# A Fourier and MLP kernel in fp32: casts of one chunk's z in later slots, accumulator copies ahead of a cast, and one block of stores split off per step

## The chip, the core and the metric

The kernel runs on one core of one Trainium2 chip. The core's engines are named here as the profile names them: PE multiplies matrices (PEld loads its stationary operand), DVE and ACT work on tiles element by element, POOL does a few small operations, and SP issues the transfers (DMAs). Each engine takes its instructions in the order in which they were written down, and waits at the head of its own queue for whatever that instruction still lacks. The metric is the device time of one execution in microseconds (us). Before the change it is 1434.35 us, the median of three runs (1433.13 to 1434.81).

## The reference

Two layer pairs, run twice, on x of 2048 rows by 512 columns. `A` mixes by Fourier matrices, `B` is a token shift with a two-layer MLP.

```python
def _A_ref(x, dft_seq_re, dft_seq_im, dft_hid_re, dft_hid_im):
    a = jnp.einsum("bsd,ed->bse", x, dft_hid_re)
    b = jnp.einsum("bsd,ed->bse", x, dft_hid_im)
    return jnp.einsum("ts,bse->bte", dft_seq_re, a) - jnp.einsum("ts,bse->bte", dft_seq_im, b)

def _B_ref(x, w1, w2, w3, w4):
    h = _gelu(_layernorm(x, axis=-1) @ w1)
    # four groups of 128 columns, shifted by +1, -1, +2, -2 rows -> hs
    x1 = x + hs @ w2
    h2 = _gelu(_layernorm(x1, axis=-1) @ w3) @ w4
    return x1 + h2

x = x + _A_ref(_layernorm(x), ...)   # layer 0
x = x + _B_ref(_layernorm(x), ...)
x = x + _A_ref(_layernorm(x), ...)   # layer 1
x = x + _B_ref(_layernorm(x), ...)
```

## The kernel before

**Precision.** Every product of two fp32 matrices is made of three matmuls: each operand is split into a high part (`hi`, a copy in the type fp32r) and a low part (`lo`, the value less its high part). `mm3` issues hi·hi, hi·lo and lo·hi into one accumulator. So each operand tile costs ACT one cast (the high part; `high`, L426, or L228, L231 and L235 for streamed weights) and DVE one subtraction (the low part; `low`, L429, or L245), and a product can start with its high parts but needs a low part at its second matmul.

**The Fourier half of a layer** works on four chunks `c` of 512 output rows. For each, `x_phase` and then `y_phase` stream pieces of the sequence matrix (`ws`, 512 KB each, tiles `raw`, four buffers) through a ring of four split tiles (`ring`, ring0f to ring3f their unsplit sums). In `y_phase` there are eight steps k, each with two items, `by1` (into accumulators PC and PD) and `by0` (into PB and PA). One step consumes one pair of pieces, and both items need both pieces (L234, a subtraction on DVE). The items run in the order k = 0 to 5, then 6 by1, 7 by1, 6 by0, 7 by0. A pair's two buffers come free when DVE has made the second item's sum, and only then may SP issue the pair after next. At the last `by1` the kernel makes im0 from PC (L517), adds to im1 (L468), casts im0 (`high(im0)`, L426) and copies PD into X1, which is part of the tile `tmp` (L523). After the loop ACT copies PB and PA into `tmp` or, in chunk 3, `beside` (L531, L533). A short hidden-dimension phase (`hid`, matmuls that read `rr`) follows chunk 3 directly.

**turned0.** In chunk 3's `y_phase` four normalised tiles of chunk 0 are transposed in blocks of 32 by DVE into `turned0` (at k = 0), stored by SP to the DRAM tile `zd` (`turn_out`: four DMAs of 256 KB, one for each block b), and loaded back as `zt0f` at k = 7 (`turn_in`, L609). The transposition is finished by the two trips together. Chunks 1, 2 and 3 get their z in the same manner later.

**by_pairs: the slots.** The first half of the MLP is 32 slots of twelve matmuls each, written out by hand. A slot is either `shifted` (z times w1, gelu on ACT at L655, cast of the gelu to `rg` at L658, its low part on DVE at L659) or `mixed` (`rg` times w2, drained by DVE at L677). A `mixed` slot takes the four `rg` of its chunk in the order 1, 3, 0, 2, so its last three matmul groups may need the `rg` made just ahead of it. Chunk 2's last `shifted` is slot 19, its first `mixed` slot 20; chunk 3's z (`zt1f`, split into `zt`) is first read in slot 23. What else runs beside a slot stands in two lists: `D(slot, ...)` is written ahead of the slot's own DVE or ACT work, `A(slot, ...)` behind it. In these lists are the casts of z (`z_highs`, `z_half`), norms (`norm3`, `ln1_of`, all L330), transposes (`turn3`, L594), stores of turned tiles (`turn_out`) and loads back (`bring`, L697; `b12`, `b22` for chunk 1). The lists alone set the order; no planner moves anything.

After the slots the MLP's second half runs over pairs of chunks, then the layer ends.

Of the kernel before, what the change touches and what calls it, by code (L numbers as in the profile page):

```python
# [14 lines left out]
S, D, F = 2048, 512, 1376  # L15
# [5 lines left out]
NC = S // CH  # L21
# [5 lines left out]
NB = P // B  # L27
# [16 lines left out]
def spectral_mlp_kernel(ctx: ExitStack, tc: tile.TileContext, x, ws, hs, w1, w2, w34, out):  # L44
# [15 lines left out]
    z3d = [dram.tile([D, CH], F32, name=f"z3d{i}") for i in range(NC)]  # L60
# [24 lines left out]
    def at(name, word, *shape, dtype=F32R):  # L85
        return nc.alloc_sbuf_tensor_at(name, [P, *shape], dtype, offset=base + 4 * word).ap()
# [11 lines left out]
    turned0 = at("turned0", 5 * AY, KD, CH, dtype=F32)  # L98
# [25 lines left out]
    def xt(j):  # L124
        return xs[j // 2][:, j % 2]
# [4 lines left out]
    count = {"mm": 0, "tmp": 0, "turn": 0}  # L130
# [24 lines left out]
    def y_order():  # L155
        order = [(k, kind) for k in range(NP) for kind in ("by1", "by0")]
        order[-3], order[-2] = order[-2], order[-3]
        return order
# [111 lines left out]
    def stream():  # L270
        i = state["use"]
        if i and items[i - 1][3] is None:
            state["done"] += 1
        state["use"] += 1
        prefetch()
        while state["two"] <= i:
            stage_two()
        return slots.pop(i)
# [137 lines left out]
    def mm_half(ps, a, slot, first, last):  # L416
        for i in range(2):
            w = slice(i * P, (i + 1) * P)
            mm3(ps[i], a[:, 0, w], a[:, 1, w], slot[:, 0], slot[:, 1], first, last)
# [5 lines left out]
    def high(tf):  # L425
        nc.scalar.copy(tf[0][:, :, 0], tf[1][:, :, 1])  # L426

    def low(tf):
        nc.vector.tensor_tensor(tf[0][:, :, 1], tf[1][:, :, 1], tf[0][:, :, 0].bitcast(F32), op=ALU.subtract)  # L429
# [37 lines left out]
    def add(o, a, b, op=ALU.add):  # L467
        nc.vector.tensor_tensor(o, a, b, op=op)  # L468

    def run_late(*names):  # L470
        for i in names:
            for f in late.pop(i, ()):
                f()
# [29 lines left out]
    def y_phase(c, hook):  # L503
        for k, kind in y_order():
            first, last = k == 0, k == NP - 1
            s = stream()
            if kind == "by1":
                hook(k)
                if k == 2:
                    run_late("y")  # L510
                if k == 4:
                    add(re0s, re0s, im1s)
                mm_half(PC, ay[k][:, 2], s[:, 0], first, last)
                mm_half(PD, ay[k][:, 0], s[:, 1], first, last)
                if last:
                    for i in range(2):
                        nc.vector.scalar_tensor_tensor(  # L517
                            im0s[:, i], PC[i], -1.0, im1s[:, i], op0=ALU.mult, op1=ALU.subtract
                        )
                    add(im1s, re0s, im0s)  # L520
                    high(im0)
                    for i in range(2):
                        nc.scalar.copy(X1[:, i], PD[i])  # L523
            else:
                if k == NP - 2:
                    low(im0)
                mm_half(PB, ay[k][:, 3], s[:, 1], first, last)
                mm_half(PA, ay[k][:, 1], s[:, 0], first, last)
        t = tmp if c < NC - 1 else beside
        for i in range(2):  # L530
            nc.scalar.copy(t[:, i], PB[i])  # L531
        for i in range(2):
            nc.scalar.copy(t[:, 2 + i], PA[i])  # L533
        late.update(
            {
                "im1-": [lambda: add(im1s, im1s, re1s, ALU.subtract)],
                "re1+": [lambda: add(re1s, re1s, t[:, 0:2]), lambda: high(re1)],
                "im1+": [lambda: add(im1s, im1s, X1), lambda: high(im1)],
                "re1": [lambda: low(re1)],
                "re0+": [lambda: add(re0s, re0s, t[:, 0:2])],  # L540
                "im1": [lambda: low(im1)],
                "re0++": [lambda: add(re0s, re0s, t[:, 2:4]), lambda: high(re0)],
                "re0": [lambda: low(re0)],
            }
        )
        if c < NC - 1:
            for i, names in enumerate((["im1-"], ["re1+"], ["im1+", "re1"], ["re0+", "im1"], ["re0++"], ["re0"])):
                late[i + 1] = [f for n in names for f in late.pop(n)]
# [43 lines left out]
    def turn_one(t, q, u):  # L592
        v = t.rearrange("p d (a q j) -> p d a q j", a=NB, q=TC)[:, :, :, q]
        nc.vector.transpose(v, blocks_of(u))  # L594

    def turn_out(t, to=None):

        if to is None:
            count["turn"] += 1
            to = zd[count["turn"] % 2]  # L600
        z = to.rearrange("(e i) t -> i e t", i=B)
        for b in range(NB):
            v = t[b * B : (b + 1) * B].rearrange("i d (a t) -> i (d a) t", a=NB)
            nc.sync.dma_start(z[:, :, b * P : (b + 1) * P], v)

# [90 lines left out]
    def b_in(c, half, to):  # L696
        nc.sync.dma_start(blkf[to][:, :, 1], z3d[c].rearrange("(h d p) t -> h p d t", h=2, p=P)[half])  # L697
# [13 lines left out]
    def z_half(c, i):  # L711
        return [t[c % 2][:, 2 * i : 2 * i + 2] for t in (zt, ztf)]

    def by_pairs(layer, zs, xin, dst):
# [14 lines left out]
        def D(slot, *fs):  # L729
            todo.setdefault((slot, 0), []).extend(fs)  # L730

        def A(slot, *fs):
            todo.setdefault((slot, 1), []).extend(fs)
# [5 lines left out]
        def u_stats(c, i, n=2):  # L739
            return lambda: mrs[c].extend(stats(x1s[c][i : i + n]))  # L740

        def add_u(c, *qs):
            return lambda: [add(xt(c * TC + q), xt(c * TC + q), x1s[c][q]) for q in qs]
# [13 lines left out]
        def turn3(t, c, *qs):  # L757
            return lambda: [turn_one(t, q, x1s[c][q]) for q in qs]
# [4 lines left out]
        def bring(c, half, to):  # L763
            return lambda: b_in(c, half, to)
# [13 lines left out]
        def z_highs(c):  # L778
            return lambda: [high(z_half(c, i)) for i in range(2)]
# [63 lines left out]
        sc0, sc1, sc2 = scratch  # L843
# [27 lines left out]
        D(14, turn(sc1, 3, 2, 3))  # L871
        A(14, lambda: turn_out(sc1))
        A(16, lambda: turn_in(ztf[1]))
        A(18, z_highs(3))
        D(21, lambda: low(z_half(3, 0)))
        D(22, lambda: low(z_half(3, 1)))

        D(6, u_stats(0, 0))
# [15 lines left out]
        D(18, add_u(1, 0, 1, 2))  # L894
        A(19, norm3(1, 0, 1, 2))
        D(19, u_stats(1, 3, 1))
        D(20, add_u(1, 3))
        D(20, turn3(sc2, 1, 0, 1, 2))
        A(20, norm3(1, 3))
        D(21, turn3(sc2, 1, 3))  # L900
        A(21, lambda: turn_out(sc2, z3d[1]))
        A(23, bring(1, 0, "12"), bring(1, 1, "22"))
        A(26, bring(0, 1, "t4"))
        D(26, sum_of("t1", "12", "t1"))
        A(27, highs("12", "22"))
# [107 lines left out]
        for pair in range(n_pairs):  # L1013
# [14 lines left out]
            if pair == 0:  # L1028
                t = tmp[:, 0:4]
# [16 lines left out]
            for i, names in enumerate((("11", "21"), ("12", "22"))):  # L1046
                for d in range(KD):
                    b = blk[names[d // 2]]
# [395 lines left out]
    for layer in range(LAYERS):  # L1444
# [4 lines left out]
        for c in range(NC):  # L1449
            if layer == 0 and c == 0:  # L1450
# [57 lines left out]
                def hook(i):  # L1508
                    k, odd = divmod(i, 2)
                    if not i:  # L1510
                        second_low(1)
                        xp_stats(1)
                        second_low(0)
                        state["two"] += 1
                        issue_dma()
                        state["limit"] = 4
                        prefetch()
                    state["limit"] = w_items[layer]
                    if not odd:
                        if k + 1 < NP:  # L1520
                            xp_norm(k + 1, 3)
                            xp_main(k + 1)
                        if not k:
                            xp_main_lows(1)
                    else:
                        if 0 < k < NP - 1:
                            xp_main_lows(k + 1)
                        if k + 2 < NP:
                            xp_stats(k + 2)
                        if k:  # L1530
                            xp_sums(k - 1)
                            xp_highs(k - 1, False)
                            xp_lows(k - 1, False)
                    w4_split(i)
# [46 lines left out]
            def hook(k):  # L1581
                if layer and c == 0:
                    for step, f in zip((1, 1, 2), (ay_sums, ay_highs, ay_lows)):
                        if k == step:
                            f(7)
                if k == 1 and c:
                    rows(X1, x1d, (c - 1) * TC + 2, 2, False)
                if c == NC - 1 and k == 0:
                    for q in range(TC):
                        turn_one(turned0, q, tmp[:, q])  # L1590
                if c == NC - 1 and k == 2:
                    turn_out(turned0)
                if c == NC - 1 and k == NP - 1:
                    turn_in(ztf[0])

# [83 lines left out]
```

## Time and profile before

| | |
|---|---|
| median of three runs | 1434.35 us (1433.13 to 1434.81) |
| the profiled execution's own time | 1434.7 us |
| its span, first to last instruction | 1432.8 us (1.9 us of its time lie around the span) |
| busy: PE, PEld, DVE, ACT, POOL | 1421.6, 1173.6, 1169.5, 730.5, 79.0 us |
| matmuls | 6261 |
| granted TensorE clock | 1.00 |
| bytes read and written in DRAM | 252.18 MB and 54.26 MB |

PE is busy nearly all the time, so whatever the change can move is found in PE's few gaps, and each gap has to be followed to the engine, and on that engine to the instruction, that came late. Busy shares of DVE and ACT are averages over stages: in `y_phase` DVE has hardly a gap, in the slots ACT has many. Layer 0 lies at 0 to about 700 us, layer 1 behind it. Chunk 3's `y_phase` is at 338 to 389 us and 1047 to 1098 us, the slots begin at 411 us and, in layer 1, near 1121 us.

### The profile page before, as it was taken

Reading aid. Unit: us, or ns where it says so; the run is one execution under the profiler, and the core shown is the slowest. Engines: PE = TensorE matmul, PEld = TensorE weight load, DVE = VectorE, ACT = ScalarE, POOL = GpSimd, SP = SyncE. Lnnn points to the kernel's source line nnn. Section 1 sums busy time; section 2 is a strip of 40 time slices with the busy share of each in tenths; the row PEclk is TensorE's granted clock in tenths of the full one; section 3 lists DMA queues with packets and bytes.
Section 4 is the critical chain, followed back from the end, with each engine's and each line's share of the span. In section 5 each row is a group of like instructions: output and inputs, shape, how many; then the busy total and the mean of one; then the engine's idle time right before and its main releaser. Section 6 shows DMA issues by size and latency. Waiting matters only on the chain.

```text
span 1432.8 us, 17313 instructions
## 1 busy us (share of the span) xinstructions
PE 1421.6 (99%) x6261; PEld 1173.6 (82%) x6261; DVE 1169.5 (82%) x1642; ACT 730.5 (51%) x992; POOL 79.0 (6%) x105
## 2 busy tenths in 40 slices
PE   9999999999999999999999999999999999999999
PEld 7888888888788788888888888888887878888887
DVE  7986998988979788656789989889988787656676
ACT  5663454455465744434555544544555665343352
POOL 2100000000002000000000000000000020000000
PEclk9999999999999999999999999999999999999999
DMA  7866656657754857944655566575676458477764
GB/s 252 276 206 205 206 192 227 210 184 267 257 162 127 276 193 264 353 157 173 216 166 191 178 233 212 172 246 188 224 273 212 141 162 294 155 244 283 243 205 161
DMA packets 127829, 307.58 MB, mean 215 GB/s; under 512 B 9216, under 2 KB 50176, under 8 KB 124544
## 3 DMA queue, kind: packets, MB, share of 16 engines
q1 hardware_dynamic: 127744, 306.48, 64.5%
q8 instruction: 49, 0.80, 0.2%
q14 instruction: 36, 0.29, 0.1%
HBM read 252.18 MB, written 54.26 MB: 214 GB/s over the span
## 4 chain that ended last, share of the span: by engine, by line
PE 90%; DVE 4%; DMA 3%; ACT 2%; issue 1%; SPq 0%; DVEq 0%; ACTq 0%
PE psd L284 9%; PE psd L282 9%; PE psd L283 9%; PE psa L284 7%; PE psa L283 7%; PE psa L282 7%; PE psc L283 7%; PE psc L284 7%; PE psc L282 7%; PE psb L283 7%; PE psb L282 7%; PE psb L284 7%; DMA raw<-in_ws 2%; DVE ring L245 1%; DMA zt1f<-zd 1%; DMA zd<-scr 1%
## 5 line engine op out<-in xcount | busy, mean ns | idle before, releaser
L228 ACT CAST ring<-raw 128x1024 fp32r<-128x1024 f32 x127 | 132.9, 1053 | 79.0 <-PE psd L284 43.0
L245 DVE TENSOR_TENSOR ring<-raw,ring 128x1024 fp32r<-128x1024 f32 x126 | 153.4, 1219 | 13.9 <-ACT ring L228 13.0
L282 PE MATMUL psd<-ring,rr 128*128 128x512 f32 x208 | 80.9, 389 | 0.0
L283 PE MATMUL psd<-ring,rr 128*128 128x512 f32 x208 | 80.9, 389 | 0.0
L284 PE MATMUL psd<-ring,rr 128*128 128x512 f32 x208 | 80.9, 389 | 0.0
L322 POOL TENSOR_TENSOR rs<-ve,mhalf 128x4 f32<-128x4 f32 x16 | 27.7, 1732 | 607.9 <-DVE nm L321 607.9
L235 ACT CAST ring<-ring0f 128x1024 fp32r<-128x1024 f32 x28 | 29.5, 1054 | 59.7 <-DVE ring0f L234 59.7
L301 POOL TENSOR_TENSOR rs<-ve,mhalf 128x2 f32<-128x2 f32 (+2 forms) x33 | 28.8, 872 | 555.5 <-DVE nb L300 555.5
L619 ACT ACTIVATE tmp<-rest 128x512 f32<-128x512 f32 x30 | 19.0, 632 | 72.9 <-DVE rest L468 72.6
L245 DVE TENSOR_TENSOR ring<-ring1f,ring 128x512 fp32r<-128x512 f32 (+1 forms) x56 | 53.3, 951 | 0.7 <-ACT ring L231 0.7
L283 PE MATMUL psc<-ring,ay 128*128 128x512 f32 x128 | 49.9, 390 | 1.2 <-DVE ring L245 1.2
L283 PE MATMUL psb<-ring,ay 128*128 128x512 f32 x128 | 50.0, 391 | 0.9 <-DVE ring L245 0.9
L330 ACT ACTIVATE tmp<-xs,nb,rs 128x512 f32<-128x512 f32 x56 | 43.3, 809 | 15.1 <-POOL nb L302 13.8
L284 PE MATMUL psb<-ring,ay 128*128 128x512 f32 x128 | 49.8, 389 | 0.0
L284 PE MATMUL psc<-ring,ay 128*128 128x512 f32 x128 | 49.8, 389 | 0.0
L282 PE MATMUL psb<-ring,ay 128*128 128x512 f32 x128 | 49.8, 389 | 0.0
L282 PE MATMUL psc<-ring,ay 128*128 128x512 f32 x128 | 49.8, 389 | 0.0
L235 ACT CAST ring<-ring1f 128x1024 fp32r<-128x1024 f32 x28 | 29.5, 1055 | 38.6 <-DVE ring1f L234 38.6
L282 PE MATMUL psa<-ring,ay 128*128 128x512 f32 x126 | 49.0, 389 | 0.0
L283 PE MATMUL psa<-ring,ay 128*128 128x512 f32 x126 | 49.0, 389 | 0.0
L284 PE MATMUL psa<-ring,ay 128*128 128x512 f32 x126 | 49.0, 389 | 0.0
L282 PE MATMUL psd<-ring,ay 128*128 128x512 f32 x126 | 49.0, 389 | 0.0
(657 smaller groups left out, 4442.2 us busy)
## 6 DMA issues: line engine op xcount, KB each, us to landing
raw<-in_ws SPq DMA_DIRECT2D x183, 512.0 KB, 5.0
w4r<-w4d SPq DMA_DIRECT2D x66, 512.0 KB, 4.7
raw<-in_hs SPq DMA_DIRECT2D x56, 512.0 KB, 3.6
w3b<-w3d SPq DMA_DIRECT2D x14, 1792.0 KB, 7.8
w3d<-w3b SPq DMA_DIRECT2D x5, 1792.0 KB, 6.9
x1d<-tmp SPq DMA_DIRECT2D x12, 512.0 KB, 6.3
xs<-x1d SPq DMA_DIRECT2D x12, 512.0 KB, 5.0
w4d<-w4in SPq DMA_DIRECT2D x11, 512.0 KB, 4.8
```

What stands on the lines that cost most here:

```text
L228: nc.scalar.copy(dest[:, a:b, 0], r[0][:, a:b])
L235: nc.scalar.copy(dest[:, :, 0], lo)
L245: nc.vector.tensor_tensor(lo, src, hi.bitcast(F32), op=ALU.subtract)
L282: nc.tensor.matmul(o, lh, rh, start=first, stop=False, skip_group_check=more)
L283: nc.tensor.matmul(o, lh, rl, start=False, stop=False, skip_group_check=more)
L284: nc.tensor.matmul(o, ll, rh, start=False, stop=last, skip_group_check=more)
L301: nc.gpsimd.tensor_tensor(rs[:, :n], ve[:, :n], mhalf[:, 0, :n], op=ALU.pow)
L322: nc.gpsimd.tensor_tensor(rs, ve, mhalf[:, :, :2], op=ALU.pow)
L330: nc.scalar.activation(o, s, AF.Identity, bias=mr[2], scale=mr[1])
L619: nc.scalar.activation(g_of, ps_of, AF.Gelu_apprx_tanh)
```

## The change

Three edits, each of which acts in both layers (the second in all eight `y_phase`s).

1. **z of chunk 3.** Its two halves were cast together in slot 18. Now half 0 is cast in slot 19 and half 1 in slot 20. DVE's low part of half 0 moves from slot 21 to 20, and chunk 1's last transpose, its store and the loads behind it move one slot on.
2. **PD.** At the end of `y_phase` the two copies of PD are written ahead of the cast of im0.
3. **turned0.** Its four stores were issued together at k = 2. Now one is issued at each of k = 2, 3, 4 and 5.

```diff
                     add(im1s, re0s, im0s)
-                    high(im0)
                     for i in range(2):
                         nc.scalar.copy(X1[:, i], PD[i])
+                    high(im0)
...
-    def turn_out(t, to=None):
+    def turn_out(t, to=None, blocks=range(NB)):
         if to is None:
-            count["turn"] += 1
+            count["turn"] += not blocks[0]
             to = zd[count["turn"] % 2]
         z = to.rearrange("(e i) t -> i e t", i=B)
-        for b in range(NB):
+        for b in blocks:
...
-        A(18, z_highs(3))
-        D(21, lambda: low(z_half(3, 0)))
+        A(19, lambda: high(z_half(3, 0)))
+        A(20, lambda: high(z_half(3, 1)))
         D(22, lambda: low(z_half(3, 1)))
...
-        D(20, add_u(1, 3))
+        D(20, add_u(1, 3), lambda: low(z_half(3, 0)))
         D(20, turn3(sc2, 1, 0, 1, 2))
         A(20, norm3(1, 3))
-        D(21, turn3(sc2, 1, 3))
-        A(21, lambda: turn_out(sc2, z3d[1]))
-        A(23, bring(1, 0, "12"), bring(1, 1, "22"))
+        D(22, turn3(sc2, 1, 3))
+        A(22, lambda: turn_out(sc2, z3d[1]))
+        A(24, bring(1, 0, "12"), bring(1, 1, "22"))
...
-                if c == NC - 1 and k == 2:
-                    turn_out(turned0)
+                if c == NC - 1 and 2 <= k < 2 + NB:
+                    turn_out(turned0, blocks=[k - 2])
```

PE's order stays as it is. On ACT, at slots 18 to 20, the casts of `zt1f` move behind the gelu and the `rg` cast of slot 19 (`gt_238` and `rg_170`) and stand among the norms; the first three rows of `rest` are chunk 1's `norm3`:

```order
 L658 CAST rg_168<-gt_236 128x512
-L426 CAST zt_142<-zt1f 128x2x512 x2
 L654 COPY gt_238<-gt_238 128x2
 L655 ACTIVATE gt_238<-psa_249 128x512
 L658 CAST rg_170<-gt_238 128x512
 L330 ACTIVATE tmp<-xs_153,nb,rs 128x512
+L426 CAST zt_142<-zt1f 128x2x512
 L330 ACTIVATE rest_240<-rest_240,nb,rs 128x512
 L330 ACTIVATE rest_241<-rest_241,nb,rs 128x512
 L330 ACTIVATE rest_242<-rest_242,nb,rs 128x512
 L330 ACTIVATE tmp<-xs_153,nb,rs 128x512
+L426 CAST zt_142<-zt1f 128x2x512
```

So slot 19's gelu no longer stands behind a cast of z. On ACT at the end of chunk 3's `y_phase`, `psd` is PD, `rr10f` is im0 and the last two rows split streamed pieces:

```order
 L228 CAST ring_176<-raw_184 128x2x512
+L522 COPY tmp<-psd_254 128x512
+L522 COPY tmp<-psd_255 128x512
 L426 CAST rr_162<-rr10f 128x2x512
-L523 COPY tmp<-psd_254 128x512
-L523 COPY tmp<-psd_255 128x512
 L228 CAST ring_178<-raw_185 128x2x512
 L228 CAST ring_180<-raw_186 128x2x512
```

The copies and the cast have changed places; nothing else moved. On SP in chunk 3's `y_phase`, `raw` are the pieces of steps 6 and 7 (a pair is 184 with 185, or 186 with 187) and `turned` is turned0:

```order
-L604 DMA zd_78<-turned_157 32x16x128 x4
-L210 DMA raw_184<-in_ws 128x1024
-L210 DMA raw_185<-in_ws 128x1024
-L210 DMA raw_186<-in_ws 128x1024
-L210 DMA raw_187<-in_ws 128x1024
+L604 DMA zd_78<-turned_157 32x16x128
+L210 DMA raw_184<-in_ws 128x1024
+L210 DMA raw_185<-in_ws 128x1024
+L604 DMA zd_78<-turned_157 32x16x128
+L210 DMA raw_186<-in_ws 128x1024
+L210 DMA raw_187<-in_ws 128x1024
+L604 DMA zd_78<-turned_157 32x16x128 x2
```

One store is still ahead of the pair for step 6, one now stands between the pairs for steps 6 and 7, and two come behind both.

## The prediction

> **What bounds the kernel now.** First the page: its first part, and the chain that ended last.
>
> ```profile
> PE 1421.6 (99%) x6261; PEld 1173.6 (82%) x6261; DVE 1169.5 (82%) x1642; ACT 730.5 (51%) x992; POOL 79.0 (6%) x105
> PE 90%; DVE 4%; DMA 3%; ACT 2%; issue 1%; SPq 0%; DVEq 0%; ACTq 0%
> ```
>
> The reader is to see that PE is the bound and that one matmul costs 1421.6 / 6261 = 0.227 us. PE's order and count stay, so this change can win only PE's gaps, and can lose only by making gaps. Next, PE's rows in the view of waits.
>
> ```profile
> PE psd L282 <- ACT rg L658: 2.6, 2, 1.4
> PE psc L283 <- DVE ring L245: 1.2, 1, 1.2
> PE psb L283 <- DVE ring L245: 0.9, 2, 0.6
> PE psb L282 <- ACT beside L531: 0.4, 1, 0.4
> ```
>
> So the gaps sit at three kinds of place: `rg` in the slots, the split of streamed pieces, the copy of PB. What each costs is read from PE's timeline, since the matmuls just behind a gap also come late:
>
> ```profile
> 374.14 0.39 PE L282 MATMUL psb<-ring,ay 128*128 128x512 f32 x1
> 375.49 0.40 PE L284 MATMUL psb<-ring,ay 128*128 128x512 f32 x1
> 389.80 0.39 PE L284 MATMUL psc<-ring,rr 128*128 128x512 f32 x1
> 390.63 0.39 PE L283 MATMUL psb<-ring,rr 128*128 128x512 f32 x1
> 467.19 0.39 PE L284 MATMUL psd<-w,rg 128*128 128x512 f32 x1
> 470.10 0.40 PE L282 MATMUL psd<-w,rg 128*128 128x512 f32 x1
> 1086.07 0.39 PE L282 MATMUL psc<-ring,ay 128*128 128x512 f32 x1
> 1088.00 0.40 PE L284 MATMUL psc<-ring,ay 128*128 128x512 f32 x1
> 1099.58 0.39 PE L284 MATMUL psc<-ring,rr 128*128 128x512 f32 x1
> 1100.69 0.39 PE L283 MATMUL psb<-ring,rr 128*128 128x512 f32 x1
> 1177.26 0.39 PE L284 MATMUL psd<-w,rg 128*128 128x512 f32 x1
> 1179.89 0.39 PE L282 MATMUL psd<-w,rg 128*128 128x512 f32 x1
> ```
>
> Each pair is the last matmul ahead of a gap and the first that is back at full pace: two starts later, four at the `rg` gaps. Less 0.227 a start, the gaps cost 0.90 (374), 0.38 (389), 2.00 (467), 1.48 (1086), 0.66 (1099) and 1.72 us (1177). Their sum, 7.14 us, is nearly all that can be won (the psb row's second wait, 0.9 - 0.6 = 0.3 us, lies at none of these places, and I leave it).
>
> **Edit 1, z of chunk 3.** The chain of waits (first row) and ACT's and DVE's timelines:
>
> ```profile
> 459.57 5.88 DMA zt1f<-zd
> 465.48 2.13 ACT L426 CAST zt<-zt1f 128x1024 fp32r<-128x1024 f32 x2 [4.01 <-DMA zt1f<-zd]
> 468.88 0.81 ACT L330 ACTIVATE tmp<-xs,nb,rs 128x512 f32<-128x512 f32 x1
> 445.11 0.69 DVE L659 TENSOR_TENSOR rg<-gt,rg 128x512 fp32r<-128x512 f32 x1 [1.03 <-ACT rg L658]
> 475.39 1.20 DVE L429 TENSOR_TENSOR zt<-zt1f,zt 128x1024 fp32r<-128x1024 f32 x1
> ```
>
> ACT stands 4.01 us for z's load and then casts for 2.13 us, with slot 19's gelu behind it. That gelu makes the `rg` for which PE waits. With the casts gone, slot 19 should look like chunk 1's slot 11, the same place eight slots earlier, where PE had no gap. There the low part ran from 445.11 to 445.80, and the high part was ready before it. Eight slots are 8 x 12 x 0.227 = 21.8 us, so in slot 20 high and low part are there at 466.9 and 467.6. PE's next matmul would start at 467.19 + 0.227 = 467.42 and needs the high part; `mixed` needs the low part two matmuls on, at 467.87. So both gaps go: 2.00 + 1.72 = 3.72 us. The bounds are 0 and 3.72, and I take the upper, because the model row has no gap.
>
> What the moved work then meets: the load has landed at 459.57 + 5.88 = 465.45. ACT is through with slot 19's `rg` near 466.9. Then a norm (0.81), half 0 (1.07), three norms (2.43), a norm (0.81), half 1 (1.07): 473.1 by full durations. Half 1's low part on DVE (1.20) ends at 474.3 or, with DVE's own queue, a little later. Slot 20 began nine matmuls ahead of 467.42, at 465.38; slot 23 begins 36 matmuls after that, at 473.55, and asks for half 1's low part at its eighth matmul, 475.14. Some 0.8 us are left; half 0 is earlier by far. The store and load of chunk 1's last turned tile stand on SP between the same neighbours, so no queue is crossed.
>
> **Edit 2, PD ahead of im0.** ACT at the end of layer 1's chunk 3, and PD's last matmul:
>
> ```profile
> 1092.41 1.06 ACT L228 CAST ring<-raw 128x1024 fp32r<-128x1024 f32 x1 [0.25 <-DMA raw<-in_hs]
> 1095.91 1.05 ACT L426 CAST rr<-rr10f 128x1024 fp32r<-128x1024 f32 x1 [2.44 <-DVE rr11f L468]
> 1096.86 1.07 ACT L523 COPY tmp<-psd 128x512 f32<-128x512 f32 x2
> 1097.81 2.01 ACT L228 CAST ring<-raw 128x1024 fp32r<-128x1024 f32 x2
> 1099.71 1.08 ACT L531 COPY beside<-psb 128x512 f32<-128x512 f32 x2
> 1092.78 0.39 PE L284 MATMUL psd<-ring,ay 128*128 128x512 f32 x1
> ```
>
> PD is complete at 1093.17, ACT free at 1093.47. The copies (1.07) fit into the 2.44 us in which ACT waits for im0, whose cast keeps its time. All behind it starts 0.95 earlier (1097.81 - 1096.86), so the first copy of PB (L531) is done near 1099.3. PE wants that bank at 1099.58 + 0.227 = 1099.81. Both gaps go, in layer 0 too, where only 0.38 is asked for: 1.04 us. Bounds 0 and 1.04; I take 1.04. In the other six phases no gap of PE stands behind these copies: nothing.
>
> **Edit 3, turned0's stores.** The chain of waits (DMAs: issue and time to landing), DVE's waits, one line's view of the pair issued at 368.8, and the landings of a pair issued at 346.6, with nothing of SP's queue beside it:
>
> ```profile
> 365.36 7.26 DMA raw<-in_ws
> 1078.58 6.55 DMA raw<-in_ws
> 372.74 1.23 DVE L234 TENSOR_TENSOR ring0f<-raw,raw 128x1024 f32<-128x1024 f32 x1 [1.65 <-DMA raw<-in_ws]
> 1085.25 1.23 DVE L234 TENSOR_TENSOR ring1f<-raw,raw 128x1024 f32<-128x1024 f32 x1 [2.03 <-DMA raw<-in_ws]
> L210 SPq DMA_DIRECT2D raw<-in_ws x2: 328/380/433, 368.8 to 369.2; - x2
> DMA to landing us min/median/max: 5.0/5.5/5.9
> DMA to landing us min/median/max: 3.9/4.4/4.8
> ```
>
> In layer 0 step 6's second piece, behind four stores, takes 7.26 us against 4.8 in quiet: 2.46 us for four stores, about 0.6 for one (an estimate). It would land by 365.36 + 4.8 + 0.6 = 370.8; DVE is ready at 372.74 - 1.65 = 371.1, so its wait goes and with it the 0.90 gap at 374. Late next is step 7's pair, now behind one store: 369.2 + 4.8 + 0.6 = 374.6 instead of 375.1. PE then asks for 6 by1's low part, which DVE makes 2.4 us after that landing (a sum and a split at 1.2 each), 377.0. PE wants it at 374.14 + 13 x 0.227 = 377.09. That is even; I count 0.8 of the 0.90. In layer 1 the late pair is step 7's: 1078.58 + 4.8 + 0.6 = 1084.0 instead of 1085.13, low part at 1086.4, wanted at 1086.07 + 0.227 = 1086.30; 0.1 to 0.2 stays and a slow start of 0.11, so 1.2 of 1.48. Together 2.0 us. Bounds: at the best 2.38; at the worst step 7's pair, with one store ahead, fares as badly as step 6's did behind four (7.26): layer 0's low part comes at 378.9, a gap of 1.9 for 0.90, layer 1's 0.7 later than now: a loss of 1.7. I take 2.0, since one store is nearest to the quiet row. SP's issues are the same four; the two stores behind step 7's pair have 10 us until the load of zt0f.
>
> **The sum.** 3.72 + 1.04 + 2.0 = 6.76. The profiled execution took 1434.7 us (span 1432.8 and 1.9 around it), so 1427.9; the median shown is 0.35 lower, so 1427.6 us. A measurement of this kernel can tell about 0.2%, 2.9 us, from no change.
>
> **Rivals.**
> - *The store's wait only moves to step 7's pair.* For: step 7's pair has a store ahead that it lacked. If its landings stay as they are (375.1, 1085.13), layer 0 wins 0.4 and layer 1 nothing: 1434.35 - 3.72 - 1.04 - 0.4 = 1429.2. With the worst bound, 1431.3. Against: the quiet row. The Trainium skill (DMA: Bandwidth & Descriptors, "Queues, rings and completion order") says that each DMA engine takes descriptors in ring order, and that a completion signal lands only after all earlier writes of that engine. By that rule step 7's pair cannot report before the store ahead has reached DRAM, which leans to 1431.3; the 7.26 us behind four stores agree with it, but no row here shows a pair with one store just ahead.
> - *The wait of the slots comes back at chunk 1's last turned tile.* It is written one slot, 2.7 us, later, and DVE sums its loaded half (`b12`):
>
> ```profile
> 487.28 1.21 DVE L468 TENSOR_TENSOR bt1f<-b12f,bt1f 128x1024 f32<-128x1024 f32 x1
> 490.72 0.69 DVE L659 TENSOR_TENSOR rg<-gt,rg 128x512 fp32r<-128x512 f32 x1 [1.63 <-ACT rg L658]
> ```
>
>   If that sum waited the whole 2.7 us, DVE's 1.63 us of slack ahead of the next `rg` would leave 1.1 in each layer: 1427.6 + 2.2 = 1429.8. Against: the tile is turned when ACT has normalised it, and ACT does that about as early as before, since it no longer stands still.
> - *Slower: the copies hold im0 up.* They wait for PD, the cast of im0 stands behind them on ACT, DVE's low part of im0 waits for the cast, and the low parts of the streamed pieces queue behind it on DVE, in all eight phases. The tightest is chunk 1 of layer 0 (ACT, DVE):
>
> ```profile
> 285.67 1.06 ACT L426 CAST rr<-rr10f 128x1024 fp32r<-128x1024 f32 x1 [0.60 <-DVE rr11f L468]
> 287.29 1.22 DVE L429 TENSOR_TENSOR rr<-rr10f,rr 128x1024 fp32r<-128x1024 f32 x1
> ```
>
>   ACT is free at 285.07, copies until 286.14, casts until 287.2; DVE comes at 287.29. If PE felt all 1.07 us in each phase, 8.6 us would stand against the 5.7 that the other edits win: 1437.2. It decides from 5.7 / 8 = 0.7 us a phase on. Against: the margin of 0.1 here, and 1.4 in the phase shown above.
>
> **Chances.** All three act: 0.66, with a range of its own of 1427.0 to 1428.8. The store's wait moves: 0.16. The slots' wait comes back: 0.11. The copies hold im0 up: 0.06. The first three are faster by over 0.2% (under 1431.5) but for their worst ends, which I put at 0.05: faster 0.88, within 0.2% 0.06, slower 0.06. The range, 1427.0 to 1430.8, takes in the first case, most of the second and the third.
>
> **What would show it.** Right: the view of waits has no row of PE for `rg` L658 and none for `beside` L531; ACT's L426 on `zt1f` has no idle time ahead of it; L522 fills ACT's idle time ahead of im0's cast; the pairs of steps 6 and 7 land near 5 us after issue. Wrong: a PE wait on `zt` in slot 23 or on `ring` L245 near 377 or 1086, DVE idle ahead of `bt1f`, or an L429 on im0 that waits for its cast in chunks 0 to 2.

## The result and the profile after

The changed kernel takes 1430.84 us, the median of 20 runs (1428.73 to 1433.08). The kernel before took 1434.2 us beside it, also over 20 runs. The ratio is 0.9978, with a 95% interval of 0.9971 to 0.9985: faster by 3.2 us (2.2 to 4.2). The forecast was 1427.6 us, and the median lies 0.04 us above the top of its range. Two of the three edits did what was forecast; the third, which was to win 2.0 us, made the kernel slower.

The profiled execution took 1428.73 us, the shortest of the 20, so its trace shows the kernel at its best. First the page's engines and its chain, then PE's rows in the view of waits, which are all that it has.

```profile
PE 1420.1 (100%) x6261; PEld 1175.2 (82%) x6261; DVE 1168.6 (82%) x1642; ACT 732.5 (51%) x992; POOL 80.6 (6%) x105
PE 94%; DVE 4%; DMA 1%; issue 0%; SPq 0%; POOL 0%; DVEq 0%; POOLq 0%
```

```profile
PE psc L283 <- DVE ring L245: 1.7, 2, 0.9
PE psd L137 <- POOL mhalf L56: 1.4, 1, 1.4
```

The rows for `rg` L658, for `beside` L531 and for `psb` and `ring` L245 are gone. The row for `psc` and `ring` L245 has grown from 1.2 us in one wait to 1.7 us in two, and the second row is the start of the program, the same in both kernels.

**Edits 1 and 2 in the trace.** ACT's timeline, around slot 19 and at the end of layer 0's `y_phase`:

```profile
465.10 0.60 ACT L655 ACTIVATE gt<-psa 128x512 f32<-128x512 f32 x1 [4.08 <-PE psa L284]
465.73 0.62 ACT L658 CAST rg<-gt 128x512 fp32r<-128x512 f32 x1
466.97 1.03 ACT L426 CAST zt<-zt1f 128x1024 fp32r<-128x1024 f32 x1
470.75 1.03 ACT L426 CAST zt<-zt1f 128x1024 fp32r<-128x1024 f32 x1
...
383.63 1.06 ACT L522 COPY tmp<-psd 128x512 f32<-128x512 f32 x2
386.06 1.05 ACT L426 CAST rr<-rr10f 128x1024 fp32r<-128x1024 f32 x1 [1.36 <-DVE rr11f L468]
388.91 1.06 ACT L531 COPY beside<-psb 128x512 f32<-128x512 f32 x2
```

The gelu ahead of slot 20 now waits for PE and not for a cast; the casts of z stand at 466.97 and 470.75 with no idle time ahead. PD's copies lie inside ACT's wait for im0, which still has 1.36 us left.

**Edit 3 in the trace.** SP's timeline, a look at the line that issues step 7's pair (with the time to landing of its two pieces), DVE's and PE's timelines in layer 0, and the same three in layer 1:

```profile
358.66 0.43 SPq L604 DMA_DIRECT2D zd<-turned  x1
364.10 0.81 SPq L210 DMA_DIRECT2D raw<-in_ws  x2
364.96 0.43 SPq L604 DMA_DIRECT2D zd<-turned  x1
368.64 0.80 SPq L210 DMA_DIRECT2D raw<-in_ws  x2
369.50 1.51 SPq L604 DMA_DIRECT2D zd<-turned  x2
```

```profile
DMA to landing us min/median/max: 5.4/5.8/6.2
375.40 1.23 DVE L234 TENSOR_TENSOR ring1f<-raw,raw 128x1024 f32<-128x1024 f32 x1 [2.24 <-DMA raw<-in_ws]
376.54 1.22 DVE L245 TENSOR_TENSOR ring<-ring0f,ring 128x1024 fp32r<-128x1024 f32 x1
376.64 0.39 PE L282 MATMUL psc<-ring,ay 128*128 128x512 f32 x1
378.14 0.39 PE L284 MATMUL psc<-ring,ay 128*128 128x512 f32 x1
...
DMA to landing us min/median/max: 5.4/5.8/6.2
1081.74 1.23 DVE L234 TENSOR_TENSOR ring1f<-raw,raw 128x1024 f32<-128x1024 f32 x1 [2.26 <-DMA raw<-in_ws]
1082.88 0.39 PE L282 MATMUL psc<-ring,ay 128*128 128x512 f32 x1
1084.49 0.40 PE L284 MATMUL psc<-ring,ay 128*128 128x512 f32 x1
```

Step 6's pair, issued at 364.10, now makes nobody wait. Step 7's pair, issued at 368.64, has a store just ahead and two just behind. Its second piece lands 6.2 us after issue in both layers. DVE waits 2.24 and 2.26 us for it, and behind that sum on DVE stands 6 by1's low part (L245 on `ring0f`), which PE needs at its next matmul. Read as in the prediction (two starts apart, less 0.227 a start), PE's gaps are 378.14 - 376.64 - 0.454 = 1.05 us and 1084.49 - 1082.88 - 0.454 = 1.16 us.

So at steps 6 and 7 these two traces are 2.38 - 2.21 = 0.2 us apart, where 2.0 were forecast. What else separates them, besides the gaps of edits 1 and 2, is not shown to come from any edit. Two parts of it can be read from DVE's and PE's timelines in the kernel before (first two rows) and from PE's in the changed kernel (third row):

```profile
1070.15 1.23 DVE L234 TENSOR_TENSOR ring0f<-raw,raw 128x1024 f32<-128x1024 f32 x1 [0.66 <-DMA raw<-in_ws]
12.34 0.39 PE L282 MATMUL psc<-ring,ay 128*128 128x512 f32 x1
12.13 0.39 PE L282 MATMUL psc<-ring,ay 128*128 128x512 f32 x1
```

In layer 1 of the kernel before, step 4's pair kept DVE waiting, and PE lost 1072.90 - 1071.87 - 0.454 = 0.57 us; the stores are issued only 5 us behind this pair, and its second piece lands 5.9 to 7.6 us after issue in layer 1 of the fourteen traces of this case, 6.6 and 6.7 in the two with no store of turned0 near. Near the program's start PE was 0.21 us later (12.34 against 12.13). 1434.7 - 3.72 - 1.04 - 0.2 - 0.57 - 0.21 is 1429.0, and 1428.73 was measured.

### The profile page after: what moved, and what is told of

It is laid out like the page before. It is cut to its first block, busy times and chain, and to the rows that moved or that the text cites. A ratio compares the mean times of both kernels' runs of the same rounds, so it can differ in the third digit from the quotient of the medians.

```text
span 1426.8 us, 17327 instructions
## 1 busy us (share of the span) xinstructions
PE 1420.1 (100%) x6261; PEld 1175.2 (82%) x6261; DVE 1168.6 (82%) x1642; ACT 732.5 (51%) x992; POOL 80.6 (6%) x105
## 4 chain that ended last, share of the span: by engine, by line
PE 94%; DVE 4%; DMA 1%; issue 0%; SPq 0%; POOL 0%; DVEq 0%; POOLq 0%
PE psd L284 9%; PE psd L282 9%; PE psd L283 9%; PE psa L282 8%; PE psa L284 8%; PE psa L283 8%; PE psc L283 7%; PE psc L284 7%; PE psc L282 7%; PE psb L282 7%; PE psb L284 7%; PE psb L283 7%; DVE ring L245 2%; DMA raw<-in_ws 1%; DVE ring2f L234 0%; DVE ring3f L234 0%
## 5 line engine op out<-in xcount | busy, mean ns | idle before, releaser
L245 DVE TENSOR_TENSOR ring<-raw,ring 128x1024 fp32r<-128x1024 f32 x126 | 153.4, 1219 | 12.8 <-ACT ring L228 12.6
L235 ACT CAST ring<-ring0f 128x1024 fp32r<-128x1024 f32 x28 | 29.5, 1054 | 56.7 <-DVE ring0f L234 56.7
L245 DVE TENSOR_TENSOR ring<-ring1f,ring 128x512 fp32r<-128x512 f32 (+1 forms) x56 | 53.2, 950 | 0.7 <-ACT ring L231 0.7
L235 ACT CAST ring<-ring1f 128x1024 fp32r<-128x1024 f32 x28 | 29.5, 1054 | 40.1 <-DVE ring1f L234 40.1
L282 PE MATMUL psd<-ring,ay 128*128 128x512 f32 x126 | 49.0, 389 | 0.0
L283 PE MATMUL psa<-ring,ay 128*128 128x512 f32 x126 | 49.0, 389 | 0.0
L283 PE MATMUL psd<-ring,ay 128*128 128x512 f32 x126 | 49.0, 389 | 0.0
L282 PE MATMUL psa<-ring,ay 128*128 128x512 f32 x126 | 49.0, 389 | 0.0
```

What stands on the lines that cost most here:

```text
L235: nc.scalar.copy(dest[:, :, 0], lo)
L245: nc.vector.tensor_tensor(lo, src, hi.bitcast(F32), op=ALU.subtract)
L282: nc.tensor.matmul(o, lh, rh, start=first, stop=False, skip_group_check=more)
L283: nc.tensor.matmul(o, lh, rl, start=False, stop=False, skip_group_check=more)
```

## The experiments

The question was which edit failed, and then by what. For edit 3 two suspects stood beside each other: the store just ahead of step 7's pair, and the stores just behind it. A third question was whether 2.38 us at steps 6 and 7 is what the kernel before usually loses there. Every kernel was run beside the kernel before (1433.29, 1434.14 and 1433.81 us, medians of the three sets).

**The changed kernel once more.**

> The changed kernel once more, unchanged, for a second trace beside its time. Its profiled execution had a span 6.0 us shorter than before's, its median is only 3.4 us lower. Theory V (the span varies with the landing of DMAs, and the first trace was a lucky one): this trace shows PE gaps of about 2 us more than the first (2.8 us in all), at waits for DMAs, in the y_phase of chunk 3 or in other y_phases, and none at rg in slot 20 and none at PB's copies. Theory S (the gaps are the same in each execution and the time is lost around the span): the same two gaps near 377 and 1083 us, 2.8 us in all, at a median near 1430.8.

1429.72 us, ratio 0.9974 (0.9964 to 0.9984). The two gaps at steps 6 and 7 are there again, 2.32 us together, and PE has no row for `rg` or `beside`. Three more gaps, near 1054, 1059 and 1071 us, together 1.5 us, are ones that the first trace lacks: that trace was a lucky one.

**Edits 1 and 2, without edit 3** (against the changed kernel):

```diff
-                if c == NC - 1 and 2 <= k < 2 + NB:
-                    turn_out(turned0, blocks=[k - 2])
+                if c == NC - 1 and k == 2:
+                    turn_out(turned0)
```

> Edits 1 and 2 without edit 3 (the four stores together at k = 2 again). If edit 3 wins in the usual execution what the two first traces show (0.90 + 1.48 + 0.58 gone, 1.06 + 1.15 new: 0.7 us): 0.7 us slower than the changed kernel, 1431.5. If edit 3 loses in the usual execution and edits 1 and 2 win their 4.76: 1429.4, that is 1.4 us faster than the changed kernel. If edits 1 and 2 win less than they seem and edit 3 does nothing: 1430.8.

1428.98 us, ratio 0.9968 (0.9956 to 0.9980): 4.6 us faster, against the forecast's 3.72 + 1.04 = 4.76. Without edit 3 the kernel is not slower but rather faster than with it (1428.98 against 1429.72 us), though the two intervals overlap. The line that issues step 7's pair and DVE's timeline behind it, in layer 0:

```profile
DMA to landing us min/median/max: 4.0/4.5/5.1
373.98 1.23 DVE L234 TENSOR_TENSOR ring1f<-raw,raw 128x1024 f32<-128x1024 f32 x1 [0.64 <-PE psd L284]
```

With the four stores together the pair lands after 5.1 us, DVE waits for PE and not for the pair, and PE has no gap at steps 6 and 7.

**Edit 1 alone** (the stores as above, and the copies of PD behind the cast):

```diff
+                    high(im0)
                     for i in range(2):
                         nc.scalar.copy(X1[:, i], PD[i])
-                    high(im0)
```

> Edit 1 alone. By the prediction it wins 3.72 us: 1430.5; the trace has no PE wait on rg in slot 20 of either layer, and the gaps at PB's copies (0.38 and 0.66) are still there. If the DMA's landing varies so that the gap before is smaller in the usual execution: 1431 to 1432.

1430.55 us, ratio 0.9976 (0.9968 to 0.9985): 3.4 us (2.1 to 4.6), against 3.72. PE has no row for `rg`, and the one for `beside` is still there (0.7 us in two waits).

**Edit 3 alone** (the kernel before, with the stores split):

```diff
-                if c == NC - 1 and k == 2:
-                    turn_out(turned0)
+                if c == NC - 1 and 2 <= k < 2 + NB:
+                    turn_out(turned0, blocks=[k - 2])
```

> Edit 3 alone. By the prediction 2.0 us faster: 1432.2. By the trace of the changed kernel, where step 7's pair comes late in both layers (gaps of 1.06 and 1.15): 0 to 0.7 us faster, 1433.5 to 1434.2. If edit 3 loses: 1435 or more. The trace shows for each layer when the pairs of steps 6 and 7 land after issue: about 4.8 us by the prediction, 5.8 to 6.2 if the trace of the changed kernel is the usual case.

1435.10 us, ratio 1.0013 (1.0003 to 1.0023): slower by 1.9 us (0.4 to 3.3). PE's waits show the gaps that the other two edits remove (first two rows), and the pair of waits that the split makes:

```profile
PE psd L282 <- ACT rg L658: 3.0, 2, 1.5
PE psb L282 <- ACT beside L531: 0.7, 2, 0.4
PE psc L283 <- DVE ring L245: 1.3, 2, 0.7
```

**Edit 2 alone** (the kernel before, with the copies ahead of the cast):

```diff
-                    high(im0)
                     for i in range(2):
                         nc.scalar.copy(X1[:, i], PD[i])
+                    high(im0)
```

> Edit 2 alone. By the prediction 1.04 us faster than before, and the trace shows no PE wait on the copies of PB (L531) in either layer, while the waits on rg stay. If ACT's freed time is taken up by something else, the same time as before and the wait still there.

1431.83 us, ratio 0.9988 (0.9979 to 0.9997): 1.7 us (0.4 to 3.0), against 1.04. PE has no row for `beside`, and the one for `rg` is still there (2.7 us in two waits).

**No store just ahead of step 7's pair, three just behind** (edits 1 and 2 stay, in this and the next two):

```diff
-                if c == NC - 1 and 2 <= k < 2 + NB:
-                    turn_out(turned0, blocks=[k - 2])
+                if c == NC - 1 and k in (2, 4):
+                    turn_out(turned0, blocks=[0] if k == 2 else [1, 2, 3])
```

> Edits 1 and 2, and of turned0's stores one ahead of step 6's pair and three behind step 7's pair; none stands between the two pairs. In the traces so far step 7's pair lands 6.3 to 6.9 us after its first issue with one store ahead and two behind, and 5.4 to 5.9 with edits 1 and 2 alone (four stores ahead of step 6's pair). Theory AHEAD (the store just ahead of a pair makes it late): 5.4 to 5.9 here, no PE gap near 375 and 1082 above 0.4, time as edits 1 and 2 alone. Theory BEHIND (stores issued just behind a pair make it late): 6.3 to 6.9 here, PE gaps of 0.9 to 1.3 there, time as the changed kernel or slower.

**One store just ahead, none behind:**

```diff
-                if c == NC - 1 and 2 <= k < 2 + NB:
-                    turn_out(turned0, blocks=[k - 2])
+                if c == NC - 1 and k in (2, 3, 7):
+                    turn_out(turned0, blocks={2: [0], 3: [1], 7: [2, 3]}[k])
```

> Edits 1 and 2, and of turned0's stores one ahead of step 6's pair, one between the pairs of steps 6 and 7, and two only at k = 7, behind the hidden-dimension pieces; none stands behind step 7's pair. Theory AHEAD: step 7's pair lands 6.3 to 6.9 us after its first issue, PE gaps of 0.9 to 1.3 near 375 and 1082. Theory BEHIND: 5.3 to 5.9, and no such gap above 0.4. In both, zt0f is loaded some us later than before, which should be hidden.

**No store near any pair** (all four at k = 7, just ahead of the load that reads them back):

```diff
-                if c == NC - 1 and 2 <= k < 2 + NB:
-                    turn_out(turned0, blocks=[k - 2])
+                if c == NC - 1 and k == 7:
+                    turn_out(turned0)
```

> Edits 1 and 2, and all four stores of turned0 only at k = 7, behind the hidden-dimension pieces, so that none of them is in flight beside the pairs of steps 5, 6 and 7. It prices the stores at these pairs. Either theory: the pairs of steps 6 and 7 land 5.2 to 5.6 us after their first issue and PE has no gap there; the load of zt0f starts some 7 us later than before and lands near 397 and 1105 instead of 389 and 1097. If that is hidden: 0 to 0.7 us faster than edits 1 and 2 alone. If ACT's cast of zt0f then waits for the load, slower by up to 2 us a layer.

The three took 1429.38 us (ratio 0.9967, 0.9956 to 0.9978), 1428.63 us (0.9965, 0.9953 to 0.9978) and 1427.12 us (0.9956, 0.9943 to 0.9968). By time alone the first two are told apart neither from each other nor from the kernel with the stores together. The landing tells more: the line that issues step 7's pair, layer 0 and then layer 1, in the three kernels in that order.

```profile
DMA to landing us min/median/max: 4.8/5.2/5.6
...
DMA to landing us min/median/max: 4.6/5.0/5.5
```

```profile
DMA to landing us min/median/max: 5.0/5.4/5.8
...
DMA to landing us min/median/max: 4.8/5.2/5.6
```

```profile
DMA to landing us min/median/max: 3.7/4.3/4.9
...
DMA to landing us min/median/max: 4.1/4.5/4.9
```

With no store near, the second piece (max) lands after 4.9 us. Three stores behind it make that 5.5 to 5.6, one store ahead 5.6 to 5.8, and one ahead with two behind, the changed kernel, 6.2. PE's gaps at steps 6 and 7, both layers together, are 1.32 us with three behind, 1.74 with one ahead and none with no store near. So neither suspect is the whole cause: each alone delays the second piece by part (0.6 to 0.7 us and 0.7 to 0.9), and together they add to about what was seen (1.3).

Step 6's pair gives a second reading of the stores behind. In the changed kernel and in the one with three stores behind step 7's pair it has the same single store ahead of it, issued some 5 us earlier; the changed kernel has one more just behind it, the other kernel has none there. The line that issues step 6's pair, layer 0 and then layer 1, first in the changed kernel, then in the other:

```profile
DMA to landing us min/median/max: 4.9/5.4/5.8
DMA to landing us min/median/max: 4.7/5.2/5.6
...
DMA to landing us min/median/max: 4.2/4.6/5.1
DMA to landing us min/median/max: 4.5/5.0/5.4
```

**The kernel before once more**, for the third question.

> The kernel before once more, for a second trace. The first showed gaps of 0.90 and 1.48 us at the pairs of steps 6 and 7 (near 374 and 1086 us). Theory OUTLIER (the first trace was a bad draw there, as the three other traces with the four stores together suggest, with 0, 0.7 and 0.7 us): 0 to 1 us in both together here, while the gaps at rg (3.7 to 4.1) and at PB's copies (1.0) are there again. Theory PLAIN (edits 1 and 2 also change what happens at these pairs): again about 2.4 us.

1434.04 us, ratio 1.0003 (0.9994 to 1.0012). PE's waits:

```profile
PE psd L282 <- ACT rg L658: 3.0, 2, 1.5
PE psb L282 <- ACT beside L531: 0.4, 1, 0.4
PE psc L283 <- DVE ring L245: 0.2, 1, 0.2
```

Its gaps at steps 6 and 7, read from PE's timeline as before, are 0.40 and 0.49 us, together 0.89. The first trace had 2.38. The waits for `rg` are nearly the same (3.0 us, and 2.6 in the first). The execution was not shorter for it: it took 1435.27 us, and the first 1434.7. One reason is not a wait. The view of windows, this trace and then the first one, shows the length of the stretch, the busy time of PE, PEld, DVE, ACT and POOL (with their instructions), the granted clock and the DMA:

```profile
1179.00:1183.00 4.00, 4.00 (x12) 3.13 (x11) 3.88 (x6) 4.00 (x7) 0.00 (x0) 0.57 0.96 352
1179.00:1183.00 4.00, 4.00 (x17) 3.00 (x18) 3.87 (x7) 4.00 (x7) 0.00 (x0) 1.00 0.84 315
```

The granted clock was 0.57 there, against 1.00, and nine of PE's matmuls took 1182.66 - 1179.01 = 3.65 us from start to start, 1.6 more than at 0.227 each.

**The changed kernel, edits 1 and 2 alone, and all stores at k = 7, each once more.**

> The changed kernel on the same chip as the next two. Gaps near 377 and 1083 us of 1.8 to 2.4 us together, as in its two earlier traces; step 7's pair lands 6.3 to 6.9 us after its first issue in both layers. Time about 1.4 us above edits 1 and 2 alone, 2.2 above the version with the stores at k = 7.

> Edits 1 and 2 alone, beside the changed kernel on the same chip: step 7's pair 5.4 to 5.9 us, gaps there 0 to 0.8 us together, 0.7 to 1.9 us faster than the changed kernel. If edit 3 costs nothing in time: the same as the changed kernel within 0.5 us.

> Edits 1 and 2 with the stores at k = 7, beside the other two on the same chip: no gap at the pairs of steps 6 and 7, landing 5.2 to 5.5 us after first issue, 6 to 7 us faster than before and 1.5 to 3 us faster than the changed kernel.

1430.80 us (0.9971, 0.9960 to 0.9983), 1428.23 us (0.9960, 0.9947 to 0.9972) and 1427.11 us (0.9955, 0.9942 to 0.9967). The order is the same as the first time, and PE's gaps at steps 6 and 7 are 2.44, 0.24 and 0.49 us. In the last one, PE shows that one gap in layer 0 although no store was near: there the second piece landed only after 5.7 us. So one such landing in four is late for a reason that these runs don't show.

All traces together: the second piece of step 7's pair, PE's gaps at steps 6 and 7 (both layers), and the second piece of step 6's pair:

| stores of turned0 | traces | step 7's landing, us | PE's gaps, us | step 6's landing, us |
|---|---|---|---|---|
| together at k = 2, first trace of before | 1 | 5.9, 6.5 | 2.38 | 7.3, 6.4 |
| together at k = 2, the others | 5 | 5.0 to 5.6 | 0.89, 0.71, 0.70, 0.24, 0 | 5.5 to 6.9 |
| one at each of k = 2 to 5 | 4 | 5.9 to 6.5 | 2.21, 2.32, 2.44, 1.81 | 5.6 to 6.5 |
| one at k = 2, three at k = 4 | 1 | 5.5, 5.6 | 1.32 | 5.1, 5.4 |
| one each at k = 2 and 3, two at k = 7 | 1 | 5.6, 5.8 | 1.74 | 5.7, 6.5 |
| all at k = 7 | 2 | 4.9, 4.9, 4.9, 5.7 | 0, 0.49 | 4.9 to 5.0 |

The mean gaps of the third row and the second are 2.2 and 0.5 us: the split costs 1.7 us. With the first trace of before counted among the traces with the stores together, their mean is 0.8, and the split costs 1.4 us. The medians agree with that roughly: with the split the kernel took 0.7 us and, in the other set, 2.6 us more than without, and edit 3 alone cost 1.9 us (0.4 to 3.3).

## Why the prediction was wrong

- **Edit 1, 3.72 us: right.** Alone it measured 3.4 us. The low part of z's half 1 was through in time, and PE has no wait on `zt` in slot 23.
- **Edit 2, 1.04 us: right.** Alone it measured 1.7 us (0.4 to 3.0). Edits 1 and 2 together gave 4.6 and 5.7 us against 4.76.
- **Edit 3, 2.0 us: wrong, and wrong in sign.** Alone it cost 1.9 us. The mechanism was drawn as it happened: step 6's wait goes, step 7's pair is late next, and 6 by1's low part stands behind its sum on DVE. The step that failed is the landing of step 7's pair, "4.8 + 0.6". The 0.6 was a quarter of what four stores had cost step 6's pair. It is 1.4 over the same quiet 4.8: 6.2 us. Those 0.8 us more fall on PE nearly one for one, since the forecast had already called the low part "even" with PE's need in layer 0 and 0.1 to 0.2 late in layer 1: it left gaps of 0.1 and 0.3 us there, and 1.05 and 1.16 were measured. The PE wait on `ring` L245 near 377, named ahead as a sign of being wrong, is there. Of the extra, one store ahead makes up 0.8 to 1.0 by itself, and the two behind, counted at nothing until the load of `zt0f`, the rest (a split that rests on the few landings above).
- **The other end of the same term.** The 2.38 us to be won were read from one trace. Five other traces with the stores together lose 0 to 0.89 us there. Even with quiet landings, edit 3 could have won about 0.5 us in the usual execution. Neither error alone would have left the range (estimates from the sums above): with the landing wrong and 2.38 us right, edit 3 wins 0.2 and the time is 1427.6 + 1.8 = 1429.4; with the landing right and 2.38 us wrong, it wins 0 to 0.5 and the time is 1429.1 to 1429.6. With both it loses 1.4 to 1.7, which gives 1431.0 to 1431.3 against the 1430.84 measured. The `rg` gaps, set by ACT's own order, are steadier (3.0 us of waits in the second trace, 2.6 in the first), and so their price held.
- **The rival that came true** is the first: the store's wait only moves to step 7's pair, 1429.2 to 1431.3 us, against 1430.84. It had a chance of 0.16. The quiet row was taken as the nearest to one store, where the rows with stores on the queue were nearer. The Trainium skill's rule there (DMA: Bandwidth & Descriptors, "Queues, rings and completion order"), that a completion lands only behind the engine's earlier writes, leaned to this rival. The changed kernel agrees in the order of events only: the time to landing of its stores in layer 0 is

```profile
L604 SPq DMA_DIRECT2D zd<-turned x4: 432/458/977, 358.7 to 370.5; - x4
DMA to landing us min/median/max: 6.3/6.3/6.5
```

  so the store issued at 364.96 lands at 371.3 to 371.5, and the pair behind it at 374.0 and 375.3. The store had landed 2.5 us before the pair's first piece, so a wait for its completion is not what made the pair late. That the stores behind a pair would delay it as well does not follow from that rule.
- **The slots' wait at chunk 1's last turned tile** does exist, but PE does not feel it. DVE's row in the view of waits:

```profile
DVE bt1f L468 <- DMA b12f<-z3d: 0.8, 1, 0.8
```

  It is shorter than DVE's slack of 1.63 us there, and PE has no row for `rg`.
- **The copies hold im0 up: no.** In the phase named as the tightest, chunk 1 of layer 0, DVE's low part of im0 runs with no wait ahead of it:

```profile
287.06 1.22 DVE L429 TENSOR_TENSOR rr<-rr10f,rr 128x1024 fp32r<-128x1024 f32 x1
```

## What to carry to other kernels

A transfer that is moved off a late load lands beside another one: ask which load of the group gates the busy engine with the least slack, and keep stores away from that one on both sides, not only ahead of it. Here step 6's pair could be late at little cost (6.9 us after issue cost PE 0.40 us in the second trace of before) and step 7's could not (6.2 us cost 1.05 and 1.16), and the best place for the stores, of those tried, was behind all loads of the loop: the kernel with edits 1 and 2 and all four stores at k = 7 takes 1427.1 us, 0.9956 of before, and beats both kernels. A gap that depends on a landing should be read from several traces before it is counted as something to win; the gaps set by an engine's own order were much alike in all the traces here.

## What was not expected of the hardware

Stores issued on the same queue *after* a pair of loads seem to delay the pair: with three stores of 256 KB right behind, two pieces of 512 KB landed 5.5 and 5.6 us after issue, against 4.9 in three of four cases with no store near (5.7 in the fourth). One store just ahead gave 5.6 and 5.8, one ahead and two behind 5.9 to 6.5 in eight landings. Step 6's pair agrees: its second piece landed after 5.6 to 6.5 us in ten landings with a store just behind, and after 5.1 and 5.4 in the two without that store. The sum of the two is firm; how it divides rests on few landings, and what makes it, shared DMA engines or the memory, was not tried.

The same place in the same kernel also varies from one execution to the next: with the stores together the gaps at steps 6 and 7 were 0.89 us in one trace of the kernel before and 2.38 us in another, while the medians of the two series (1434.04 and 1434.2 us) are the same.
